# Attention with its first four steps pinned to program order on two engines, its loads in another order, and GpSimd's weight preparation cut into 256-column pieces

## The chip, the cores and the metric

The kernel runs on one core of a Trainium2 chip. The core has five engines that run side by side and wait for each other by semaphores: TensorE (PE; its weight loads stand in rows of their own as PEld), VectorE (DVE), ScalarE (ACT), GpSimd (POOL) and SyncE (SP), which here only issues transfers. The metric is the device time of one execution in microseconds, the median of several.

## The reference, cut to what matters

Attention with sinks and a window, then two mixtures of experts, one after the other, all in float32:

```python
# attention: B, H, S, D = 2, 8, 768, 64; n_sink = 4, window = 128
scores = scale * (q @ k.T)
keep = (pos[None, :] < n_sink) | ((rel >= 0) & (rel < window))
a = softmax(where(keep, scores, -1e9));  x = a @ v          # 1536 tokens of 512
# first mixture: each token goes to one of 8 experts, greedily by its logit, 192 tokens an expert
out[mask] = relu(x[mask] @ w1[e]) @ w2[e]
# second mixture: every token through every expert, weighted by P from 8 Sinkhorn rounds
out += P[:, e:e + 1] * (relu(x @ w1[e]) @ w2[e])
```

## The kernel before

**Attention** works on 12 chunks of 128 tokens (6 for each of two batches) in 15 steps `c`. A step works on four chunks at once, each at another stage. For chunk `c`, PE multiplies queries with keys (`scores`, tile S, 8 heads as two halves of two head pairs) and DVE adds the mask and takes the maximum (`negmax` closes the step). For chunk `c-1`, ACT takes the exponential in place (`expo`, tile pb). For chunk `c-2`, PE transposes the exponentials (`pt`, PSUM tile PT, copied by ACT to the tile pt) and multiplies them with the values (`pv`, PSUM tile o) for the first two head pairs. For chunk `c-3`, `pv` does the other two pairs, ACT copies the sum (`xt`), and `xn` multiplies with an identity that carries the gate's weights (tile xr). In the same step `turn(c+1, "k")` and `turn(c+1, "q")` transpose the next chunk's keys and queries on PE, through one PSUM buffer with the tag "tr" that `turn`, the sinks and the first half of `xn` share. ACT copies the keys out of it (tile KT), DVE the queries (qt).

A scheduler puts the instructions of each engine in an order of its own choice, by its own estimates; the program text gives the dependences and the priority alone. Each engine then works through its own list strictly in that order.

`load(c)` has SP issue three transfers of 256 KB for chunk c: keys, queries, values. Keys and queries have 3 buffers each, values 5. `load_sinks(b)`, in the steps 1 and 7, loads the values of the four sink tokens and makes of them (a matmul by `spread`, a product and three copies on DVE) the tile vs, which chunk 2 of a batch is the first to use. Ahead of all of them on SP stands the gate of the second mixture, wg2.

**Routing and the first mixture** follow: 8 rounds that each choose an expert and its tokens, gather them and run the expert (`moe1`, lines 736 and 747). At the end of a round `operands` makes the sums T1 to T4 and splits each of them into a high and a low part (lines 699 to 707). DVE does the sums and the low parts, each with two inputs in SBUF.

**The second mixture** walks over 32 pieces of weights ("chunks" `(e, i)`) with two token blocks each: 64 units. `first(u)` makes the hidden values by seven products (tiles X, Y, Z; `hidden`, tile h), `second(u-1)` the outputs (tile pa), alternately on PE. `prepare(e, i)` fetches a piece's weights and splits them into a high part by ACT and a low part by POOL. It is a generator that is stepped between the products. Its subtractions on POOL are one of 512, one of 256 and two of 1024 columns for each piece (lines 460 and 477); before them come four small ones of 256 columns (lines 462 to 465, tile S). During the first units the Sinkhorn rounds run too (lines 808 to 819): DVE sums rows, PE sums columns (tile gmx), DVE scales.

```python
        def parts(o, n, x):
            nc.scalar.activation(w1[0][:, o:o + n], x, AF.Copy)
            nc.gpsimd.tensor_sub(w1[1][:, o:o + n], x, w1[0][:, o:o + n].bitcast(F32))
```

Of the kernel before, what the change touches and what calls it, by code (L numbers as in the profile page):

```python
# [8 lines left out]
F32 = mybir.dt.float32  # L9
# [3 lines left out]
AF = mybir.ActivationFunctionType  # L13
# [7 lines left out]
def kernel(  # L21
# [16 lines left out]
    nc = tc.nc  # L38
    B, H, S, D = q.shape
    N, DM = out.shape  # L40
    E = moe_w_gate.shape[1]
    F = moe_w1.shape[2]
    P = 128
    NI = S // P
    NCH = N // P
    NP = H // 2
# [26 lines left out]

    rcx = ExitStack()
    rp = rcx.enter_context(tc.tile_pool(name="rt", bufs=1, side="right"))
    nc.sync.dma_start(wg2, moe2_w_gate.rearrange("(k p) e -> p k e", p=P))
    nc.vector.memset(ones, 1.0)
    NC2 = NCH // 2
    ji = rp.tile([P, NC2 * P], I32, name="ji", tag="row")
# [44 lines left out]
    def attention():  # L124
# [8 lines left out]

        KT = [ap.tile([P, NP, NI, RW], F32, name=f"KT{b}", bufs=1) for b in range(B)]

        def load(c):
            b, i = divmod(c, NI)
            for name, store, src in (("kn", KN, k), ("qn", QN, q), ("vn", VN, v)):
                t = ap.tile([P, H, D], F32, name=name, bufs=5 if name == "vn" else 3)
                nc.sync.dma_start(t, src[b, :, i * P:(i + 1) * P, :].rearrange("h s d -> s h d"))  # L140
                store[c] = t

        SB_ = 4
        load(0)
        load(1)
        load(2)
        identr = ap.tile([P, P], F32R, name="identr", bufs=1)
        nc.vector.tensor_copy(identr, ident)

# [42 lines left out]
                       channel_multiplier=0)  # L192
        nc.vector.tensor_scalar(spread, jr[:NS, :P], pf[:NS, 0:1], None, op0=OP.is_equal)

        def load_sinks(b):

            vn = ap.tile([NS, H, D], F32, name="vsn")
            nc.sync.dma_start(vn, v[b, :, 0:NS, :].rearrange("h s d -> s h d"))
            pt = pp.tile([P, DM], F32, name="tr", bufs=1)
            nc.tensor.matmul(pt, spread, vn.rearrange("s h d -> s (h d)"), start=True, stop=True)  # L200
            vf = ap.tile([P, DM], F32, name="vf", tag="vf", bufs=1)
            nc.vector.tensor_mul(vf, pt, diag)
            t = VS[b] = ap.tile([P, DM], F32R, name="vs")
            nc.vector.tensor_copy(t, vf)
            for g in (1, 3):
                r = slice(g * H * NS, (g + 1) * H * NS)
                nc.vector.tensor_sub(t[r], vf[r], t[r].bitcast(F32))

        def turn(c, which):

            b, i = divmod(c, NI)
            x = (QN if which == "q" else KN).pop(c)
            pt = pp.tile([P, NP, P], F32, name="tr", bufs=1)
            for hp in range(NP):
                nc.tensor.transpose(pt[:, hp, :], x[:, 2 * hp:2 * hp + 2, :].rearrange("p s d -> p (s d)"), ident)  # L215
            if which == "q":
                QT[c] = ap.tile([P, NP, P], F32, name="qt")
                nc.vector.tensor_copy(QT[c], pt)
            else:
                nc.scalar.activation(KT[b][:, :, i, :P], pt, AF.Copy)  # L220
                nc.vector.tensor_copy(KT[b][:, :, i, P:], KT[b][:, :, 0, 0:NS])

        def dims(c):
# [3 lines left out]
        def scores(c, hp):  # L227
            i, nt, w = dims(c)
            if hp == 0:
                NB[c] = ap.tile([P, 4, H], F32, name="nb", bufs=4)  # L230
                PB[c] = ap.tile([P, H, 2 * RW], F32, name="pb", bufs=3)
            mask = M0 if i == 0 else (M1 if i == 1 else M2).rearrange("p t j -> p (t j)")
            ps = [pp.tile([P, 512], F32, name="S", bufs=SB_) for _ in range(2)]

            for s in range(2):
                r = slice(s * D, (s + 1) * D)
                kk = KT[c // NI][r, hp, i, :P] if i == 0 else \
                    KT[c // NI][r, hp, i - 1:i + 1, :].rearrange("p t j -> p (t j)")
                nc.tensor.matmul(ps[s][:, :w], QT[c][r, hp, :], kk, start=True, stop=True)  # L239
            for s in range(2):  # L240
                h = 2 * hp + s
                nc.vector.tensor_tensor_reduce(PB[c][:, h, :w], ps[s][:, :w], mask, scale=1.0, scalar=-3.0e38,  # L242
                                               op0=OP.add, op1=OP.max, accum_out=NB[c][:, 0, h:h + 1])

        def negmax(c, h0=0, h1=H):
            nb = NB[c]
            nc.vector.tensor_scalar(nb[:, 0, h0:h1], nb[:, 0, h0:h1], -scale, None, op0=OP.mult)  # L247

        def expo(c, hp):
            i, nt, w = dims(c)  # L250
            for h in (2 * hp, 2 * hp + 1):
                nc.scalar.activation(PB[c][:, h, :w], PB[c][:, h, :w], AF.Exp, bias=NB[c][:, 0, h:h + 1], scale=scale,  # L252
                                     accum_out=NB[c][:, 2, h:h + 1])

        def recip(c):
            nb = NB[c]
# [5 lines left out]
        def pt_sinks(c):  # L262
            i, nt, w = dims(c)
            if i < 2:
                return
            sp = PB[c][:, :, w - NS:].unsqueeze(1).to_broadcast([P, 2, H, NS])
            sb = ap.tile([P, 2, 2, H, NS], F32R, name="psn")
            nc.vector.tensor_copy(sb[:, 0], sp)
            nc.vector.tensor_sub(sb[:, 1], sp, sb[:, 0].bitcast(F32))
            pm = pp.tile([P, 4, P], F32R, name="PT", bufs=2)  # L270
            nc.tensor.transpose(pm[:, 0, :], sb.rearrange("p a b h j -> p (a b h j)"), identr)
            PS[c] = ap.tile([P, P], F32R, name="pst")
            nc.vector.tensor_copy(PS[c], pm[:, 0, :].bitcast(F32))

        def sinks(c):

            OT[c] = pp.tile([P, NP, P], F32, name="o", bufs=1)
            if c % NI >= 2:
                for hp in range(NP):
                    nc.tensor.matmul(OT[c][:, hp, :], VS[c // NI][:, hp * P:(hp + 1) * P], PS[c], start=(hp == 0),  # L280
                                     stop=False, skip_group_check=True)

        def pt(c, hp):
            i, nt, w = dims(c)
            pm = pp.tile([P, 4, P], F32, name="PT", bufs=2)
            for s in range(2):
                for t in range(nt):
                    nc.tensor.transpose(pm[:, s * nt + t, :], PB[c][:, 2 * hp + s, t * RW:t * RW + P], ident)  # L288
            PT[c, hp] = ap.tile([P, 4, P], F32, name="pt", bufs=4)
            nc.scalar.activation(PT[c, hp][:, :2 * nt], pm[:, :2 * nt], AF.Copy)  # L290

        def pv(c, hp):
            i, nt, w = dims(c)
            b = c // NI
            o = OT[c]
            for t in range(nt):
                for s in range(2):
                    nc.tensor.matmul(o[s * D:(s + 1) * D, hp, :], VN[c - nt + 1 + t][:, 2 * hp + s, :],  # L298
                                     PT[c, hp][:, s * nt + t, :], start=(i < 2 and t == 0), stop=(t == nt - 1),
                                     skip_group_check=True)  # L300

        def xt(c):
            XT[c] = ap.tile([P, NP, P], F32, name="xt")
            nc.scalar.activation(XT[c], OT[c], AF.Copy)

        def xn(c):

# [2 lines left out]
            for h0 in range(0, H, 4):  # L310
                pt_ = pp.tile([P, 2, P + 2 * E], F32, name="xr", **(dict(tag="PT", bufs=2) if h0 else dict(tag="tr", bufs=1)))
                for a in range(2):
                    nc.tensor.matmul(pt_[:, a], XT[c][:, h0 // 2 + a, :], wbd[:, h0 // 2 + a], start=True, stop=True)  # L313
                den = NB[c][:, 3, h0:h0 + 4].rearrange("p (a s) -> p a s", s=2).unsqueeze(3)
                nc.vector.tensor_mul(lp[:, h0:h0 + 4].rearrange("p (a s) e -> p a s e", s=2),
                                     pt_[:, :, P:].rearrange("p a (s e) -> p a s e", s=2),
# [54 lines left out]
        masks()  # L371
        for c in range(NCH + 3):
            c1, c2, c3 = (c - j if 0 <= c - j < NCH else None for j in (1, 2, 3))
            cur = c < NCH
            if c + 3 < NCH:
                load(c + 3)
            if c % NI == 1 and cur:
                load_sinks(c // NI)
            if c2 is not None:
                recip(c2)  # L380
# [32 lines left out]
                        first_round(c3)  # L413
            if cur and c < NCH - 1:
                negmax(c)
        first_count()
        return cx

# [26 lines left out]
    def prepare(e, i):  # L445
# [11 lines left out]

        def parts(o, n, x):
            nc.scalar.activation(w1[0][:, o:o + n], x, AF.Copy)  # L459
            nc.gpsimd.tensor_sub(w1[1][:, o:o + n], x, w1[0][:, o:o + n].bitcast(F32))  # L460

        nc.gpsimd.tensor_add(S[:, 0], A21, A22)
        nc.gpsimd.tensor_sub(S[:, 1], S[:, 0], A11)
# [10 lines left out]
        nc.sync.dma_start(r2, moe2_w2[e, fs, :].rearrange("(k p) d -> p k d", p=P))  # L474
        w2 = bp.tile([P, 2, FP, DM], F32R, name="w2", tag="w", bufs=WB)
        nc.scalar.activation(w2[:, 0], r2, AF.Copy)  # L476
        nc.gpsimd.tensor_sub(w2[:, 1], r2, w2[:, 0].bitcast(F32))  # L477
        WC[e, i] = w1, w2

    def run(steps):  # L480
# [307 lines left out]
    def moe2(cx):  # L788
# [132 lines left out]
        for n in range(len(units) + 1):  # L921
# [8 lines left out]
            for k in (5, 2):  # L930
                for _ in range(k):
                    next(a, None)
                    if n > 1:
                        next(sk, None)
                next(prep, None)
                for j in range(TB):
                    next(b, None)
                    if n > 1:
                        next(sk, None)
                    if j < 2:  # L940
                        next(prep, None)

    cx = routing_and_moe1()
# [35 lines left out]
```

## Time and profile before

| | us |
|---|---|
| median of 3 runs | 1403.85 |
| lowest and highest | 1403.66, 1405.28 |
| the profiled execution, its own time | 1406.31 |
| its span, from the first to the last instruction | 1404.6 |
| attention, about | 0 to 145 |
| routing and the first mixture, about | 145 to 386 |
| second mixture, about | 386 to 1404 |

The profile is of one execution. 1.7 us of its time lie outside of the span. It took 2.5 us longer than the median run, 0.18%. A row of the timeline gives the start, the duration, the engine, the source line and the tiles (out<-in); "[1.18 <-DVE qt L218]" behind it is the time for which the engine stood idle before it, and what ended that.

### The profile page before, as it was taken

The page shows a single profiled execution, that of the slowest core. Times are in us where ns is not written, and L with a number is a line of the kernel's source. Part 1 is how long each engine was busy: PE and PEld are TensorE (multiplying, and loading weights), DVE is VectorE, ACT ScalarE, POOL GpSimd, SP SyncE. Part 2 cuts the span into 40 slices and gives each one's busy share as a digit, 9 for nine tenths or more (in the row PEclk, how much of TensorE's full clock was granted, in tenths as well). Part 3 has the DMA queues.
Part 4 walks back from the last instruction along what each step waited for, and adds up shares of the span by engine and source line. Part 5 has one row for each costly group of instructions (what it writes and reads, how often), then busy time and mean ns, then how long its engine had stood idle before and what let it go on. Part 6 is the DMA issues. An engine that isn't in the chain of part 4 may idle for free.

```text
span 1404.6 us, 20726 instructions
## 1 busy us (share of the span) xinstructions
PE 1361.5 (97%) x8195; PEld 1220.9 (87%) x8195; DVE 810.7 (58%) x1921; ACT 458.5 (33%) x975; POOL 405.4 (29%) x388
## 2 busy tenths in 40 slices
PE   7999599999989999999999999999999999999998
PEld 4677499999988989998999899988998999989987
DVE  4777778860357655555555555555555555555554
ACT  4766111222343333333323233323232333232321
POOL 1146301011342222232333223323332233233203
PEclk8999699999999999999999999999999999999999
DMA  5431434668210000011010000110100001011002
GB/s 122 112 78 39 147 132 154 225 184 225 77 46 30 31 31 31 30 35 42 30 45 31 31 31 30 40 36 31 45 31 30 31 30 44 32 31 45 1 1 90
DMA packets 87225, 87.37 MB, mean 62 GB/s; under 512 B 43864, under 2 KB 60248, under 8 KB 87128
## 3 DMA queue, kind: packets, MB, share of 16 engines
q1 hardware_dynamic: 82056, 73.45, 17.0%
q0 software_dynamic: 2944, 9.44, 1.9%
q10 hardware_dynamic: 2128, 3.16, 0.6%
q8 instruction: 64, 1.05, 0.3%
q14 instruction: 33, 0.27, 0.1%
HBM read 79.75 MB, written 6.30 MB: 61 GB/s over the span
## 4 chain that ended last, share of the span: by engine, by line
PE 90%; DVE 4%; ACT 2%; POOL 2%; issue 1%; POOLq 0%; DVEq 0%; ACTq 0%
PE pa L895 36%; PE X L838 19%; PE Z L838 9%; PE mm L736 6%; PE mm L747 6%; PE Y L838 5%; PE S L239 2%; ACT pb L252 1%; PE o L298 1%; PE cnt L584 1%; PE PT L288 1%; POOL G L355 1%; PE tr L215 1%; PE xr L313 1%; DVE pb L242 1%
## 5 line engine op out<-in xcount | busy, mean ns | idle before, releaser
L895 PE MATMUL pa<-w,h 128*128 128x512 f32 x2304 | 548.7, 391 | 0.0
L895 PEld LDWEIGHTS pa<-w,h 128*128 128x128 f32 x2304 | 430.3, 188 | 85.0
L906 DVE SCALAR_TENSOR_TENSOR accs<-pa,Pm,accs 128x512 f32<-128x512 f32 x360 | 270.1, 750 | 135.0 <-PE pa L895 133.2
L477 POOL TENSOR_TENSOR w<-r,w 128x1024 fp32r<-128x1024 f32 x32 | 77.1, 2409 | 392.1 <-ACT w L476 392.1
L846 DVE SCALAR_TENSOR_TENSOR h<-sum,h 128x384 fp32r<-128x384 f32 x192 | 128.4, 669 | 58.2 <-ACT h L845 58.1
L845 ACT ACTIVATE h<-sum 128x384 fp32r<-128x384 f32 x192 | 100.5, 523 | 158.8 <-DVE sum L855 158.8
L460 POOL TENSOR_TENSOR w1l<-r,w1h 128x512 fp32r<-128x512 f32 x64 | 64.3, 1026 | 294.1 <-ACT w1h L459 285.3
L845 ACT ACTIVATE h<-X 128x384 fp32r<-128x384 f32 x64 | 31.5, 492 | 214.2 <-PE X L838 214.2
L736 PE MATMUL mm<-xe,wf 128*128 128x192 f32 x512 | 95.9, 337 | 0.0
L855 DVE TENSOR_TENSOR sum<-Z,u 128x384 f32<-128x384 f32 x64 | 35.7, 558 | 104.4 <-ACT u L850 104.4
L747 PE MATMUL mm<-hT,wf 128*128 128x192 f32 x512 | 91.5, 331 | 0.0
L855 DVE TENSOR_TENSOR sum<-Y,p 128x384 f32<-128x384 f32 x64 | 35.7, 557 | 89.1 <-PE Y L838 89.1
L460 POOL TENSOR_TENSOR w1l<-S,w1h 128x1024 fp32r<-128x1024 f32 x32 | 86.6, 2707 | 0.0
L736 PEld LDWEIGHTS mm<-xe,wf 128*128 128x128 f32 x512 | 83.2, 192 | 0.1
L747 PEld LDWEIGHTS mm<-hT,wf 128*128 128x128 f32 x512 | 82.6, 190 | 0.5
L846 DVE SCALAR_TENSOR_TENSOR h<-X,h 128x384 fp32r<-128x384 f32 x64 | 35.7, 558 | 53.8 <-ACT h L845 53.8
L850 ACT ACTIVATE p<-X 128x384 f32<-128x384 f32 x64 | 31.5, 491 | 107.2 <-PE X L838 105.4
L684 POOL DMA_INDIRECT xg<-X,ixs x16 | 16.4, 1023 | 168.6 <-PE mm L720 60.6
L850 ACT ACTIVATE u<-X 128x384 f32<-128x384 f32 x64 | 31.5, 493 | 100.9 <-PE X L838 100.9
L476 ACT ACTIVATE w<-r 128x1024 fp32r<-128x1024 f32 x32 | 34.0, 1062 | 88.1 <-PE pa L895 88.1
L252 ACT ACTIVATE pb<-pb,nb 128x264 f32<-128x264 f32 (+1 forms) x96 | 46.3, 486 | 14.1 <-DVE nb L247 14.1
L738 ACT ACTIVATE hT<-mm 128x384 f32<-128x384 f32 x32 | 15.7, 491 | 78.7 <-PE mm L736 78.6
(282 smaller groups left out, 2324.7 us busy)
## 6 DMA issues: line engine op xcount, KB each, us to landing
r<-in_moe_w_dram SPq DMA_DIRECT2D x64, 512.0 KB, 3.4
wf<-in_moe_w_dram SPq DMA_DIRECT2D x29, 1024.0 KB, 7.8
kn<-in_k_dram SPq DMA_DIRECT2D x12, 256.0 KB, 3.9
qn<-in_q_dram SPq DMA_DIRECT2D x12, 256.0 KB, 2.9
vn<-in_v_dram SPq DMA_DIRECT2D x12, 256.0 KB, 3.4
X<-xs POOLq DMA_DIRECT2D x12, 256.0 KB
wf<-in_moe_w_dram ACTq DMA_DIRECT2D x3, 1024.0 KB, 10.4
xg<-X,ixs POOLq DMA_INDIRECT x16
```

The source lines that it names most:

```text
L252: nc.scalar.activation(PB[c][:, h, :w], PB[c][:, h, :w], AF.Exp, bias=NB[c][:, 0, h:h + 1], scale=scale, accum_out=NB[c][:, 2, h:h + 1])
L460: nc.gpsimd.tensor_sub(w1[1][:, o:o + n], x, w1[0][:, o:o + n].bitcast(F32))
L477: nc.gpsimd.tensor_sub(w2[:, 1], r2, w2[:, 0].bitcast(F32))
L736: nc.tensor.matmul(ph[:, j - j0, :], w1[j // JH][:, k, j % JH * P:(j % JH + 1) * P], xe[:, k, :], start=(k == 0), stop=(k == KD - 1))
L747: nc.tensor.matmul(py[:, k - k0, :], w2[j // JH][:, j % JH, k * P:(k + 1) * P], hT[:, j, :], start=(j == 0), stop=(j == KF - 1))
L838: nc.tensor.matmul(acc_, w1[a][:, o, k, :], XO[x][t][b][:, k, :], start=(start and n == 0), stop=(stop and n == 3 * KH - 1), skip_group_ch ...
L845: nc.scalar.activation(t[:, 0], x, AF.Relu)
L846: nc.vector.scalar_tensor_tensor(t[:, 1], x, 0.0, t[:, 0].bitcast(F32), op0=OP.max, op1=OP.subtract)
L850: nc.scalar.activation(t, x, AF.Copy)
L855: nc.vector.tensor_add(t, a, b)
L895: nc.tensor.matmul(pa, HT[u, f, h][:, a, j * P:(j + 1) * P], w2[:, b, f, :], start=(n == 0), stop=(n == 3 * FP - 1))
L906: nc.vector.scalar_tensor_tensor(acc[:, c], pa, pe, acc[:, c], op0=OP.mult, op1=OP.add)
```

## The change

Five things change. (1) In the steps 0 to 3 each instruction of PE and ACT gets an ordering edge to the one that the program issued before it on that engine (`inorder`), so that in these steps both follow the program text; from step 4 on the scheduler is free again. (2) The loads: keys and queries of chunks 0 and 1 go first, the values of a chunk one place later, and wg2 after the values of chunk 2. (3) The queries of chunk 0 are transposed into a buffer of the tag "S" and not into the one that the keys stand in. (4) The sinks' load is issued in the steps 0 and 6 and their matmul and DVE work move to the end of steps 3 and 9 (`make_sinks`). (5) POOL's subtractions in `prepare` go in pieces of 256 columns, 11 where there were 4; and `prepare` isn't stepped in the first unit.

```diff
-        load(0)
-        load(1)
-        load(2)
+        load(0, "kq")
+        load(1, "kq")
+        load(0, "v")
+        load(2, "kq")
+        load(1, "v")
+        load(2, "v")
+        nc.sync.dma_start(wg2, moe2_w_gate.rearrange("(k p) e -> p k e", p=P))
...
+        FILL = 3
+        last = {}
+
+        def inorder(op):
+            i = op.ins
+            if i.engine in last:
+                if last[i.engine] is not None:
+                    tc.add_manual_dep(i, last[i.engine].name, mybir.DependencyInfo(
+                        mybir.DependencyClass.NoSync, mybir.DependencyReason.DATA), reason="in order")
+                last[i.engine] = i
+
+        last.update({mybir.EngineType.PE: None, mybir.EngineType.Activation: None})
...
-            pt = pp.tile([P, NP, P], F32, name="tr", bufs=1)
+            pt = pp.tile([P, NP, P], F32, name="tr", **(dict(tag="S", bufs=SB_) if c == 0 and which == "q" else
+                                                        dict(tag="tr", bufs=1)))
...
+            if c > FILL:
+                last.clear()
...
-            if c % NI == 1 and cur:
+            if c % NI == 0 and cur:
                 load_sinks(c // NI)
...
+            if c % NI == 3 and cur:
+                make_sinks(c // NI)
...
-            nc.gpsimd.tensor_sub(w1[1][:, o:o + n], x, w1[0][:, o:o + n].bitcast(F32))
+            for j in range(n):
+                nc.gpsimd.tensor_sub(w1[1][:, o + j], x[:, j], w1[0][:, o + j].bitcast(F32))
...
-        nc.gpsimd.tensor_sub(w2[:, 1], r2, w2[:, 0].bitcast(F32))
+        for f in range(FP):
+            for h in range(2):
+                d = slice(h * DM // 2, (h + 1) * DM // 2)
+                nc.gpsimd.tensor_sub(w2[:, 1, f, d], r2[:, f, d], w2[:, 0, f, d].bitcast(F32))
...
-                next(prep, None)
+                if n:
+                    next(prep, None)
```

PE in attention, from the second half of the scores of chunk 0 on. Before:

```order
L239 MATMUL S<-KT_126,qt 128x128 x4
L215 MATMUL tr<-ident,qn 128x128 x4
L288 MATMUL PT<-ident,pb 128x128
L239 MATMUL S<-KT_126,qt 128x264 x8
L288 MATMUL PT<-ident,pb 128x128 x3
L298 MATMUL o<-pt,vn 64x128 x2
```

Now:

```order
L263 MATMUL S<-KT_125,qt 128x128 x4
L239 MATMUL tr<-ident,qn 128x128 x4
L263 MATMUL S<-KT_125,qt 128x264 x4
L239 MATMUL tr<-ident,kn 128x128 x4
L263 MATMUL S<-KT_125,qt 128x264 x4
L239 MATMUL tr<-ident,qn 128x128 x4
L263 MATMUL S<-KT_125,qt 128x264 x4
L239 MATMUL tr<-ident,kn 128x128 x4
L312 MATMUL PT<-ident,pb 128x128 x4
```

The transposes of chunk 2's keys and queries and the scores of chunk 2 stood behind all of chunk 0's and most of chunk 1's later work and behind the sinks' matmul; now they come directly after the scores of chunk 1.

ACT over the same steps (KT is the copy of a chunk's keys, pb the exponentials, pt the copy of transposed ones, xt that of a chunk's sum). Before:

```order
L220 ACTIVATE KT_126<-tr 128x4x128 x2
L252 ACTIVATE pb,nb<-pb,nb 128x128 x8
L290 ACTIVATE pt<-PT 128x256 x2
L252 ACTIVATE pb,nb<-pb,nb 128x264 x8
L290 ACTIVATE pt<-PT 128x256 x2
L304 ACTIVATE xt<-o 128x512
```

Now:

```order
L244 ACTIVATE KT_125<-tr 128x4x128 x2
L276 ACTIVATE pb,nb<-pb,nb 128x128 x4
L244 ACTIVATE KT_125<-tr 128x4x128
L276 ACTIVATE pb,nb<-pb,nb 128x128 x4
L276 ACTIVATE pb,nb<-pb,nb 128x264 x4
L244 ACTIVATE KT_125<-tr 128x4x128
L314 ACTIVATE pt<-PT 128x256 x2
L276 ACTIVATE pb,nb<-pb,nb 128x264 x4
L314 ACTIVATE pt<-PT 128x256 x2
L328 ACTIVATE xt<-o 128x512
```

The eight exponentials of chunk 1 stood in one block ahead of the second copy of chunk 0's transposes; now they stand in two blocks of four, with the copies between them.

POOL, the second piece of weights of the second mixture, about where the first mixture ends. Before:

```order
L460 TENSOR_TENSOR w1l<-S,w1h 128x1024
L462 TENSOR_TENSOR S<-r_5122 128x256
L464 TENSOR_TENSOR S<-r_5122 128x256
L463 TENSOR_TENSOR S<-S,r_5122 128x256
L465 TENSOR_TENSOR S<-r_5122,S 128x256
L477 TENSOR_TENSOR w_4939<-r_4937,w_4939 128x1024
```

Now:

```order
L489 TENSOR_TENSOR w1l<-S,w1h 128x256 x4
L491 TENSOR_TENSOR S<-r_5136 128x256
L493 TENSOR_TENSOR S<-r_5136 128x256
L492 TENSOR_TENSOR S<-S,r_5136 128x256
L494 TENSOR_TENSOR S<-r_5136,S 128x256
L509 TENSOR_TENSOR w_5051<-r_5049,w_5051 128x256 x4
```

The sequence is the same, with four short subtractions in the place of each long one. Behind attention the lists of PE, ACT, DVE and SP are the same as before, in the first unit of the second mixture too.

## Rows read from the trace of the kernel before

**Rows 1.** The page, its head.
```profile
span 1404.6 us, 20726 instructions
```
**Rows 2.** Windows: length, busy PE, PEld, DVE, ACT, POOL, PE's granted clock, DMA share, GB/s.
```profile
530.00:1000.00 470.00, 470.00 (x2353) 424.72 (x2352) 257.87 (x393) 146.82 (x271) 149.11 (x120) 1.00 0.10 34
```
**Rows 3.** Waits of PE: us in total, times, longest us.
```profile
PE Y L838 <- DVE sum L855: 4.2, 1, 4.2
...
PE o L298 <- ACT pt L290: 3.1, 1, 3.1
...
PE gmx L816 <- DVE cs L812: 2.2, 2, 1.5
```
**Rows 4.** Windows of attention's first steps.
```profile
20.00:25.00 5.00, 1.91 (x15) 1.34 (x14) 0.38 (x2) 4.05 (x17) 0.00 (x0) 0.72 0.00 0
25.00:30.00 5.00, 5.00 (x19) 2.61 (x18) 1.46 (x3) 1.59 (x3) 0.00 (x0) 0.50 0.00 0
```
**Rows 5.** Timeline of attention's first steps, SP, PE, DVE and ACT.
```profile
0.81 0.44 SPq L76 DMA_DIRECT2D wg<-in_moe_w_gate_dram  x1
1.30 0.50 SPq L140 DMA_DIRECT2D kn<-in_k_dram  x1
...
4.94 1.08 PE L215 MATMUL tr<-ident,kn 128*128 128x128 f32 x4 [4.94 <-POOL jr L187]
...
6.71 1.11 PE L215 MATMUL tr<-ident,qn 128*128 128x128 f32 x4 [0.69 <-ACT KT L220]
...
7.86 0.69 DVE L218 COPY qt<-tr 128x512 f32<-128x512 f32 x1 [0.61 <-PE tr L215]
...
13.22 0.39 ACT L252 ACTIVATE pb<-pb,nb 128x128 f32<-128x128 f32 x1
...
13.86 4.26 PE L239 MATMUL S<-KT,qt 64*128 64x264 f32 x16
...
25.90 0.60 ACT L290 ACTIVATE pt<-PT 128x512 f32<-128x512 f32 x1 [0.50 <-PE PT L288]
...
44.95 1.16 PE L239 MATMUL S<-KT,qt 64*128 64x264 f32 x8
...
53.85 0.71 PE L239 MATMUL S<-KT,qt 64*128 64x264 f32 x2
```
**Rows 6.** The chain that ended last, attention's first steps: start, us, what.
```profile
19.34 3.98 ACT pb L252 x16
```
**Rows 7.** Timeline of PE where the sinks of batch 1 stand now.
```profile
76.08 1.12 PE L200 MATMUL tr<-vsn,spread 4*128 4x512 f32 x2
```
**Rows 8.** The chain that ended last, the second mixture's first units.
```profile
387.34 2.65 DVE T L701
389.99 1.02 DVE T L702
...
394.04 2.61 DVE xT4l L707
...
449.29 2.40 DVE h L846
```
**Rows 9.** Timeline of POOL and DVE over the same units.
```profile
386.89 2.69 POOL L460 TENSOR_TENSOR w1l<-S,w1h 128x1024 fp32r<-128x1024 f32 x1
...
390.56 1.05 POOL L464 TENSOR_TENSOR S<-r 128x256 f32<-128x256 f32 x1
...
398.08 0.56 DVE L846 SCALAR_TENSOR_TENSOR h<-sum,h 128x384 fp32r<-128x384 f32 x1 [0.59 <-ACT h L845]
...
418.99 0.74 POOL L464 TENSOR_TENSOR S<-r 128x256 f32<-128x256 f32 x1
...
448.88 2.40 POOL L460 TENSOR_TENSOR w1l<-S,w1h 128x1024 fp32r<-128x1024 f32 x1
```
**Rows 10.** Windows of the clock in the second mixture's first units.
```profile
397.00:402.00 5.00, 4.46 (x16) 4.31 (x17) 1.43 (x4) 1.78 (x4) 0.00 (x0) 0.66 0.52 106
455.00:460.00 5.00, 4.90 (x20) 4.90 (x21) 4.07 (x12) 1.01 (x2) 0.00 (x0) 0.66 0.01 3
```

More of the change, by code (lines that the diff above doesn't have):

```diff
@@ L75 @@
     rp = rcx.enter_context(tc.tile_pool(name="rt", bufs=1, side="right"))
-    nc.sync.dma_start(wg2, moe2_w_gate.rearrange("(k p) e -> p k e", p=P))
     nc.vector.memset(ones, 1.0)
@@ L134, in attention, with load @@
         KT = [ap.tile([P, NP, NI, RW], F32, name=f"KT{b}", bufs=1) for b in range(B)]
-        def load(c):
+        def load(c, kinds="kqv"):
             b, i = divmod(c, NI)
             for name, store, src in (("kn", KN, k), ("qn", QN, q), ("vn", VN, v)):
+                if name[0] not in kinds:
+                    continue
                 t = ap.tile([P, H, D], F32, name=name, bufs=5 if name == "vn" else 3)
@@ L193, in attention, with make_sinks @@
         nc.vector.tensor_scalar(spread, jr[:NS, :P], pf[:NS, 0:1], None, op0=OP.is_equal)
+        VSN = {}
         def load_sinks(b):
-            vn = ap.tile([NS, H, D], F32, name="vsn")
-            nc.sync.dma_start(vn, v[b, :, 0:NS, :].rearrange("h s d -> s h d"))
+            VSN[b] = ap.tile([NS, H, D], F32, name="vsn")
+            nc.sync.dma_start(VSN[b], v[b, :, 0:NS, :].rearrange("h s d -> s h d"))
+        FILL = 3
[8 more added lines that the diff above has]
+        last.update({mybir.EngineType.PE: None, mybir.EngineType.Activation: None})
+        def make_sinks(b):
+            vn = VSN.pop(b)
             pt = pp.tile([P, DM], F32, name="tr", bufs=1)
-            nc.tensor.matmul(pt, spread, vn.rearrange("s h d -> s (h d)"), start=True, stop=True)
+            inorder(nc.tensor.matmul(pt, spread, vn.rearrange("s h d -> s (h d)"), start=True, stop=True))
             vf = ap.tile([P, DM], F32, name="vf", tag="vf", bufs=1)
@@ L212, in turn @@
             x = (QN if which == "q" else KN).pop(c)
-            pt = pp.tile([P, NP, P], F32, name="tr", bufs=1)
+            pt = pp.tile([P, NP, P], F32, name="tr", **(dict(tag="S", bufs=SB_) if c == 0 and which == "q" else
+                                                        dict(tag="tr", bufs=1)))
             for hp in range(NP):
-                nc.tensor.transpose(pt[:, hp, :], x[:, 2 * hp:2 * hp + 2, :].rearrange("p s d -> p (s d)"), ident)
+                inorder(nc.tensor.transpose(pt[:, hp, :], x[:, 2 * hp:2 * hp + 2, :].rearrange("p s d -> p (s d)"), ident))
             if which == "q":
@@ L219, in turn @@
             else:
-                nc.scalar.activation(KT[b][:, :, i, :P], pt, AF.Copy)
+                inorder(nc.scalar.activation(KT[b][:, :, i, :P], pt, AF.Copy))
                 nc.vector.tensor_copy(KT[b][:, :, i, P:], KT[b][:, :, 0, 0:NS])
@@ L238, in scores @@
                     KT[c // NI][r, hp, i - 1:i + 1, :].rearrange("p t j -> p (t j)")
-                nc.tensor.matmul(ps[s][:, :w], QT[c][r, hp, :], kk, start=True, stop=True)
+                inorder(nc.tensor.matmul(ps[s][:, :w], QT[c][r, hp, :], kk, start=True, stop=True))
             for s in range(2):
@@ L251, in expo @@
             for h in (2 * hp, 2 * hp + 1):
-                nc.scalar.activation(PB[c][:, h, :w], PB[c][:, h, :w], AF.Exp, bias=NB[c][:, 0, h:h + 1], scale=scale,
-                                     accum_out=NB[c][:, 2, h:h + 1])
+                inorder(nc.scalar.activation(PB[c][:, h, :w], PB[c][:, h, :w], AF.Exp, bias=NB[c][:, 0, h:h + 1], scale=scale,
+                                     accum_out=NB[c][:, 2, h:h + 1]))
         def recip(c):
@@ L270, in pt_sinks @@
             pm = pp.tile([P, 4, P], F32R, name="PT", bufs=2)
-            nc.tensor.transpose(pm[:, 0, :], sb.rearrange("p a b h j -> p (a b h j)"), identr)
+            inorder(nc.tensor.transpose(pm[:, 0, :], sb.rearrange("p a b h j -> p (a b h j)"), identr))
             PS[c] = ap.tile([P, P], F32R, name="pst")
@@ L279, in sinks @@
                 for hp in range(NP):
-                    nc.tensor.matmul(OT[c][:, hp, :], VS[c // NI][:, hp * P:(hp + 1) * P], PS[c], start=(hp == 0),
-                                     stop=False, skip_group_check=True)
+                    inorder(nc.tensor.matmul(OT[c][:, hp, :], VS[c // NI][:, hp * P:(hp + 1) * P], PS[c], start=(hp == 0),
+                                     stop=False, skip_group_check=True))
         def pt(c, hp):
@@ L287, in pt @@
                 for t in range(nt):
-                    nc.tensor.transpose(pm[:, s * nt + t, :], PB[c][:, 2 * hp + s, t * RW:t * RW + P], ident)
+                    inorder(nc.tensor.transpose(pm[:, s * nt + t, :], PB[c][:, 2 * hp + s, t * RW:t * RW + P], ident))
             PT[c, hp] = ap.tile([P, 4, P], F32, name="pt", bufs=4)
-            nc.scalar.activation(PT[c, hp][:, :2 * nt], pm[:, :2 * nt], AF.Copy)
+            inorder(nc.scalar.activation(PT[c, hp][:, :2 * nt], pm[:, :2 * nt], AF.Copy))
         def pv(c, hp):
@@ L297, in pv @@
                 for s in range(2):
-                    nc.tensor.matmul(o[s * D:(s + 1) * D, hp, :], VN[c - nt + 1 + t][:, 2 * hp + s, :],
+                    inorder(nc.tensor.matmul(o[s * D:(s + 1) * D, hp, :], VN[c - nt + 1 + t][:, 2 * hp + s, :],
                                      PT[c, hp][:, s * nt + t, :], start=(i < 2 and t == 0), stop=(t == nt - 1),
-                                     skip_group_check=True)
+                                     skip_group_check=True))
         def xt(c):
             XT[c] = ap.tile([P, NP, P], F32, name="xt")
-            nc.scalar.activation(XT[c], OT[c], AF.Copy)
+            inorder(nc.scalar.activation(XT[c], OT[c], AF.Copy))
         def xn(c):
@@ L312, in xn @@
                 for a in range(2):
-                    nc.tensor.matmul(pt_[:, a], XT[c][:, h0 // 2 + a, :], wbd[:, h0 // 2 + a], start=True, stop=True)
+                    inorder(nc.tensor.matmul(pt_[:, a], XT[c][:, h0 // 2 + a, :], wbd[:, h0 // 2 + a], start=True, stop=True))
                 den = NB[c][:, 3, h0:h0 + 4].rearrange("p (a s) -> p a s", s=2).unsqueeze(3)
@@ L939, in moe2 @@
                         next(sk, None)
-                    if j < 2:
+                    if n and j < 2:
                         next(prep, None)
```

## The prediction, made before the run

> **What bounds the kernel now.** I read the page's head first (a span of 1404.6 us [rows 1]), then windows by stage, then PE's waits, and only then the timeline. In the second mixture PE has no gap: it is busy for 470.00 of 470 us from 530 to 1000 [rows 2]. So time can only be won or lost there if PE is made to wait, and no edit takes work from PE. The reader should look at PE's own waits. Most of the long ones lie where this change acts: 3.1 us in attention, on ACT's copy pt; 4.2 us in the first unit of the second mixture, on DVE's sum; 2.2 us in two waits of the Sinkhorn rounds for DVE's column sums [rows 3]. Each has a second price, which is no wait: after it PE's granted clock falls to 0.50, the level of 1.2 GHz, for some us [rows 4]. Its matmuls then take nearly twice as long and look busy.
>
> **Attention before.** The scores of chunk 1 begin at 13.86, those of chunk 4 at 44.95 [rows 5]: 31.1 us for three steps that hold less work than a late one, and the step that begins at 44.95 takes 8.9. The reason stands in the chain: ACT does all eight exponentials of chunk 1 (19.34 to 23.32) [rows 6] before it copies the transposes that PE waits for. PE is idle for 3.1 us, its clock goes to 0.50, and from 25 to 30 it is "busy" at that level [rows 3, 4], with the sinks' matmul among it.
>
> **Attention now, worked out step by step.** Start: wg2's issue ahead of the first keys goes, 1.30 − 0.81 = 0.49. The queries' transposes began at 6.71, when ACT had emptied the one buffer; they can now begin when the keys' end, 4.94 + 1.08 = 6.02, if the queries have landed: 0.69 more [rows 5]. Together 1.2 us for the first scores. The next chain (two halves of scores, two turns) keeps most of it; I take 1.0, so chunk 1's scores begin at 12.9.
>
> Now I follow the pinned lists, whichever engine ends last. As slow as in the rows of the start, four transposes take 1.1 (at 6.71) and half of a chunk's scores 4.26/2 = 2.1; ACT's 512-column copies (KT, pt, xt) take 0.6, one of half that size I put at 0.3; an exponential of chunk 0 0.39, of a later chunk 3.98/8 = 0.50 (the chain counts each with its read-out) [rows 5, 6].
> - Step 1, from 12.9: PE half of scores 2.1, key transposes 1.1, other half 2.1, query transposes 1.1; then DVE's copy qt 0.69 [rows 5]. 7.1, so step 2 begins at 20.0. ACT must hold the second half of chunk 0's exponentials until the keys' copy is done (16.1 + 0.6), 4 × 0.39 = 1.6, done at 18.3: hidden.
> - Step 2: ACT sets the end. Exponentials 2.0, keys 0.6, two short copies 0.6, exponentials 2.0; then DVE, in whose list the first part of the reciprocal, which needs all eight sums, stands ahead of qt: 0.2 + 0.7. 6.1, so step 3 begins at 26.1.
> - Step 3: PE scores 1.16 and the last products of chunk 0, about 0.5; ACT xt 0.6, exponentials 2.0, keys 0.6, two copies 1.2, exponentials 2.0 beside which PE does products, transposes and the first half of xr, about 1.1 more until the next scores. 9.1, so chunk 4's scores begin at 35.2, 9.8 earlier than before.
>
> Here PE is taken to be at the higher level from step 2 on, since step 1 keeps it busy for 6.4 us on end.
>
> What is owed then: half of chunk 1's products with the values, about 0.6, which the list before had done by 44.95; and the sinks, whose matmul holds PE for 1.1 where it stood in batch 1 [rows 7]. Their other move, step 7 to step 9, takes 1.1 out and puts it back. So attention wins 9.8 − 0.6 − 1.1 = 8.1. From step 4 on PE has few gaps, routing needs attention's last logits, and the first mixture's weights are fetched by expert number, after routing; so I carry it to the end unshortened. For sinks the loads come in steps 0 and 6, three steps ahead of need; wg2 is needed only after routing: nothing. Values one place later (about 1.1 us of transfer each) land before 14, and chunk 0's are first used after 22: nothing; if a value tile were late, PE would wait in step 2 behind it, at most by 1.
>
> **The second mixture's start.** At 387.34 a DVE sum T takes 2.65 in the chain, and at 394.04 a low part takes 2.61 [rows 8]. Both lie under one long POOL subtraction (386.89, 2.69) [rows 9] or its like; both have two inputs in SBUF. Between them DVE's same operations take 1.02 from start to start, while POOL runs 256-column operations that themselves take 1.05 [rows 8, 9]: the two alternate. After the change all of POOL's operations there have that size, so six DVE operations take 6 × 1.02 in place of 2.65 + 4 × 1.01 + 2.61: 3.2 us sooner, and PE's wait of 4.2 shrinks to 1.0. Then the clock: over the 5 us after that wait it is 0.66 of full [rows 10], which costs 5 × 0.34 = 1.7; this comes back if the short wait doesn't lower it. Sum 4.9.
>
> The Trainium skill, page "SBUF — State Buffer", section "Who interferes with whom", says that a DVE instruction with two SBUF inputs and a GpSimd instruction exclude each other for the whole instruction. By it, alternating operations would add up, 0.56 for DVE's alone and 0.74 for POOL's alone [rows 9]: 1.30 a pair; six would take 7.8, this term would be 3.2 and the time 1390. The measured 1.02 of the same operations decides.
>
> The second place is DVE's h at 449.29: 2.40 under a POOL subtraction of 2.40 [rows 8, 9]. With pieces it takes 1.02, 1.4 less; the small Sinkhorn operations around it lose a little, since POOL works longer. I take 1.3 of PE's 2.2 [rows 3], and again 5 × 0.34 = 1.7 for the clock after it [rows 10]. Sum 3.0.
>
> Elsewhere pieces cost nothing: a long subtraction becomes four of at most 1.05, some 2 us more POOL time in two units of 16 us (1018 us over 64), where POOL is busy for a third [rows 2]. If the low parts came too late PE would wait on them; they are done a unit ahead. Stepping `prepare` one unit later changes no list: nothing.
>
> **Sum:** 8.1 + 4.9 + 3.0 = 16.0. Against the span 1404.6 that is 1388.6, against the execution's own 1406.3 it is 1390.3; the median run was 2.5 below the profiled one, so I forecast 1403.85 − 16.0 = **1387.8 us**.
>
> **Rivals.**
> (a) *PE stays at the lower level through steps 2 and 3.* The pinned lists make PE wait for ACT in both. At that level scores take 0.9 more a half; each set of transposes I estimate at 0.5 more (half of the start's 1.1), products as much: about 8 us for two steps, of which the gaps absorb half. Attention wins 4, the time is 1392. For it: in rows 4 it sat at 0.50 while busy. Against: gaps worked out here are near 1 us, that one 3.1.
> (b) *The written order takes the gain back.* ACT idles in the lists, some 2 us before the copy of chunk 2's keys and 2 before xt; if each further hand-over costs as much, steps 2 and 3 take 10 us each and more, attention wins 2 and the time is 1394. Against: the later steps, bound by the same hand-overs, take about 9.
> (c) *Pieces don't do what they are for:* POOL holds on through a run of four, DVE waits as long as before. Only attention wins: 1396. Against: the alternation in rows 8 and 9.
> (d) *Slower.* In the second mixture's steady part each piece blocks a two-input DVE operation, more often than one long one did; if DVE's h came late by 0.3 us of PE's time in each of 62 units, 18.6 us would go, more than all gains: 1406. Against: there PE has no gap now and DVE is busy for 55% [rows 2]; it decides only if h has less slack than one piece, some 1 us.
>
> **How the numbers follow.** Forecast, give or take 3.5 (the start 0.6 either way, the second fall of the clock 1.7, hand-overs 1 each): 0.56. (a) 0.18, (b) 0.14, (c) 0.09, (d) 0.03. The range of 8 in 10 goes from 1383.5, all terms at their upper ends, to 1396, which holds (a), (b) and most of (c). About 0.2% (2.8 us) is what a measurement of this kernel tells from no change. All but (d) end below 1401: faster 0.94; between its price and the gains lies little, same 0.03, slower 0.03.
>
> **What would show it.** Chunk 4's scores near 35; no window at 0.50 between 20 and 33; ACT's exponentials in fours. Around 379, DVE's T and low parts at about 1.0, none at 2.6; PE's wait for sum near 1.0; granted clock 1.00 after it; likewise for h near 435. PE still without a gap in the steady units. If chunk 4's scores come after 39 with the clock at 0.50, (a); with it at 1.00, (b). If DVE's long ones stay, (c).

## The result and the profile after

The changed kernel takes 1388.73 us in the median (1387.02 to 1390.14) against 1404.57 for the kernel before, four executions of each, a ratio of 0.9883 (interval 0.9871 to 0.9896). The forecast was 1387.8, in a range from 1383.5 to 1396. The profiled execution took 1387.89 us.

The waits of PE show first what is gone (columns: what waits, for what, us in total, times, longest):

```profile
PE S L263 <- DVE qt L242: 4.0, 4, 1.2
...
PE Y L870 <- DVE sum L887: 1.6, 1, 1.6
PE o L322 <- ACT pt L314: 1.1, 1, 1.1
...
PE gmx L848 <- DVE cs L844: 0.3, 1, 0.3
```

The three waits of [rows 3] have shrunk, 4.2 to 1.6, 3.1 to 1.1 and 2.2 to 0.3. Of the four waits for DVE's copy of the queries one was there before, ahead of chunk 0's scores (0.8); three are new, at the start of steps 1 to 3 as the prediction followed them. The windows at about the same places of the program (columns as in rows 2):

```profile
20.00:25.00 5.00, 3.87 (x39) 2.54 (x36) 3.56 (x17) 2.92 (x12) 0.00 (x0) 1.00 0.91 205
25.00:30.00 5.00, 3.91 (x39) 3.02 (x40) 2.15 (x13) 4.97 (x17) 0.00 (x0) 1.00 0.26 58
385.00:390.00 5.00, 5.00 (x28) 4.79 (x29) 3.00 (x6) 1.93 (x5) 2.51 (x4) 1.00 0.27 78
435.00:440.00 5.00, 5.00 (x28) 4.41 (x27) 3.86 (x13) 0.72 (x2) 4.84 (x8) 1.00 0.28 105
520.00:990.00 470.00, 470.00 (x2353) 424.69 (x2352) 261.03 (x393) 147.45 (x272) 166.72 (x225) 1.00 0.11 35
```

The reader should look at the sixth figure behind the window's length, PE's granted clock: 1.00 in all five, where [rows 4, 10] had 0.72, 0.50, 0.66 and 0.66. And the last row has no gap of PE in the steady units, with POOL at 166.72 us in place of 149.11.

Attention's scores, in PE's timeline (start, duration):

```profile
12.45 1.16 PE L263 MATMUL S<-KT,qt 64*128 64x264 f32 x8 [0.78 <-DVE qt L242]
...
17.21 1.16 PE L263 MATMUL S<-KT,qt 64*128 64x264 f32 x8 [1.17 <-DVE qt L242]
...
23.23 1.16 PE L263 MATMUL S<-KT,qt 64*128 64x264 f32 x8 [1.13 <-DVE qt L242]
...
31.82 0.71 PE L263 MATMUL S<-KT,qt 64*128 64x264 f32 x2
```

These are the first scores of chunks 1 to 4; those of chunk 4 begin 13.1 us earlier than in [rows 5]. At the second mixture's start DVE and POOL read so:

```profile
375.86 1.11 DVE L732 TENSOR_TENSOR T<-yT,T 128x384 f32<-128x384 f32 x1 [3.50 <-ACT yT L781]
376.89 1.08 DVE L733 TENSOR_TENSOR T<-yT 128x384 f32<-128x384 f32 x1
377.90 1.09 DVE L734 TENSOR_TENSOR T<-yT,T 128x384 f32<-128x384 f32 x1
...
381.95 1.08 DVE L739 TENSOR_TENSOR xT4l<-T,xT4h 128x384 fp32r<-128x384 f32 x1
...
383.32 0.55 DVE L887 TENSOR_TENSOR sum<-Y,p 128x384 f32<-128x384 f32 x1
...
433.86 0.82 DVE L878 SCALAR_TENSOR_TENSOR h<-sum,h 128x384 fp32r<-128x384 f32 x1
```
```profile
376.50 4.10 POOL L489 TENSOR_TENSOR w1l<-S,w1h 128x256 fp32r<-128x256 f32 x4
```

No DVE operation takes 2.6 any more: each of the sums and low parts begins 1.01 to 1.03 behind the one before it, while POOL does its four pieces in 4.10. The h that took 2.40 [rows 8] takes 0.82.

### The profile page after: what moved, and what is told of

It reads as the page before. It is cut to its first block, busy times and chain, and to the rows that moved or that the text cites. A ratio compares the mean times of both kernels' runs of the same rounds, so it can differ in the third digit from the quotient of the medians.

```text
span 1386.2 us, 20957 instructions
## 1 busy us (share of the span) xinstructions
PE 1349.7 (97%) x8195; PEld 1213.9 (88%) x8195; DVE 811.0 (59%) x1921; ACT 458.2 (33%) x975; POOL 443.3 (32%) x612
## 4 chain that ended last, share of the span: by engine, by line
PE 92%; DVE 4%; ACT 2%; issue 1%; POOL 1%; DMA 0%; POOLq 0%; SPq 0%; DVEq 0%; ACTq 0%
PE pa L927 37%; PE X L870 19%; PE Z L870 9%; PE mm L768 6%; PE mm L779 6%; PE Y L870 5%; PE S L263 2%; ACT pb L276 1%; PE o L322 1%; PE cnt L616 1%; PE PT L312 1%; PE xr L337 1%; DVE pb L266 1%; PE tr L239 1%; POOL out_dram L940 1%
## 5 line engine op out<-in xcount | busy, mean ns | idle before, releaser
L509 POOL TENSOR_TENSOR w<-r,w 128x256 fp32r<-128x256 f32 x128 | 90.4, 739 | 365.8 <-ACT w L505 365.8
L878 DVE SCALAR_TENSOR_TENSOR h<-sum,h 128x384 fp32r<-128x384 f32 x192 | 136.4, 711 | 58.1 <-ACT h L877 57.9
L489 POOL TENSOR_TENSOR w1l<-r,w1h 128x256 fp32r<-128x256 f32 x96 | 68.6, 743 | 275.1 <-ACT w1h L487 267.1
L489 POOL TENSOR_TENSOR w1l<-S,w1h 128x256 fp32r<-128x256 f32 x128 | 102.7, 832 | 0.0
```

The lines of the kernel that those rows point to most:

```text
L489: nc.gpsimd.tensor_sub(w1[1][:, o + j], x[:, j], w1[0][:, o + j].bitcast(F32))
L509: nc.gpsimd.tensor_sub(w2[:, 1, f, d], r2[:, f, d], w2[:, 0, f, d].bitcast(F32))
L878: nc.vector.scalar_tensor_tensor(t[:, 1], x, 0.0, t[:, 0].bitcast(F32), op0=OP.max, op1=OP.subtract)
```

## The experiments

Each was timed beside the kernel before on the same chip. The first four take the change apart.

**Whole subtractions again.** The changed kernel, with POOL's eleven pieces as four operations.

```diff
-            for j in range(n):
-                nc.gpsimd.tensor_sub(w1[1][:, o + j], x[:, j], w1[0][:, o + j].bitcast(F32))
+            nc.gpsimd.tensor_sub(w1[1][:, o:o + n], x, w1[0][:, o:o + n].bitcast(F32))
...
+        nc.gpsimd.tensor_sub(w2[:, 1], r2, w2[:, 0].bitcast(F32))
```

> The changed kernel with GpSimd's subtractions of the weight preparation whole again (512, 256, 1024, 1024 columns); attention stays as changed. Theory (DVE's two-input operations wait for a long POOL operation to end): the two waits at the start of the second mixture come back, so about 7 us of the 16 go: 1396, PE's wait for sum near 4, a DVE sum T and a low part at 2.6, the granted clock 0.50 after it. Rival (they met only because attention ended at an unlucky moment, and the earlier end of attention alone parts them): no DVE operation over 1.1, the time stays near 1389.

1395.36, ratio 0.9929 (0.9916 to 0.9943) to the kernel before. The waits came back (waits of PE, then DVE's timeline, then two windows):

```profile
PE Y L866 <- DVE sum L883: 4.2, 1, 4.2
...
PE gmx L844 <- DVE cs L840: 2.2, 2, 1.5
```
```profile
377.57 2.73 DVE L729 TENSOR_TENSOR T<-yT 128x384 f32<-128x384 f32 x1
...
384.27 2.69 DVE L735 TENSOR_TENSOR xT4l<-T,xT4h 128x384 fp32r<-128x384 f32 x1
```
```profile
385.00:390.00 5.00, 2.15 (x7) 2.15 (x8) 3.32 (x5) 1.28 (x3) 1.54 (x1) 0.77 0.50 106
446.00:451.00 5.00, 5.00 (x28) 4.70 (x27) 4.57 (x12) 1.85 (x4) 0.00 (x0) 1.00 0.01 3
```

So an earlier end of attention doesn't part the two engines; the pieces do. But the last window, right behind the wait of 1.5 for the column sums, is at 1.00, where [rows 10] had 0.66 behind the same wait.

**Pieces alone.** The kernel before with the pieces of the change and nothing else.

> The kernel before with the subtractions in pieces of 256 columns and nothing else. Theory: 7 us faster, 1397, all of it between the first sum T of the second mixture and its fourth unit; attention as before. Rival (the gain of the pieces hangs on the other edits): under 2 us faster, 1402 or more.

1397.99, ratio 0.9952 (0.9938 to 0.9965): 6.2 us by the medians. PE waits for sum for 1.6 us and for the column sums for 0.3, as in the changed kernel. The pieces need nothing of the other edits.

**No ordering edges.** The changed kernel without the line that switches them on.

```diff
-        last.update({mybir.EngineType.PE: None, mybir.EngineType.Activation: None})
```

> The changed kernel without the ordering edges; loads, buffer, moved sinks and pieces stay. Theory as predicted (the pinned order wins in attention): most of attention's gain goes, 1396 or more, chunk 4's scores after 40. Rival (the sinks' matmul, which waited for a late load with the one buffer that the transposes need, was what held the order back, and its move alone lets the scheduler find nearly the written order): within 2 us of the changed kernel, 1387 to 1391, chunk 4's scores between 31 and 35.

1388.67, ratio 0.9886 (0.9871 to 0.9901), the same as the changed kernel. PE's timeline, chunks 1 and 4:

```profile
11.74 1.16 PE L262 MATMUL S<-KT,qt 64*128 64x264 f32 x8
...
31.31 0.71 PE L262 MATMUL S<-KT,qt 64*128 64x264 f32 x2
```

The scheduler, left free, is no later than the written order. My theory of the pins falls here. The rival's time and its mark in the trace are met; that the sinks' move is the reason is for the next run to show.

**The sinks' move alone.** The kernel before, with the sinks' load and matmul moved and nothing else.

```diff
-            if c % NI == 1 and cur:
+            if c % NI == 0 and cur:
                 load_sinks(c // NI)
...
+            if c % NI == 3 and cur:
+                make_sinks(c // NI)
```

> The kernel before with the sinks' load and matmul moved and nothing else: no ordering edges, old order of loads, old buffer, whole subtractions. Theory as predicted (the sinks' move costs and gains nothing, the pins bring the gain): 1402 to 1405. Rival (the move alone brings most of attention's gain): 1393 to 1396, chunk 4's scores before 37, no stretch at a granted clock of 0.50 between 20 and 33.

1395.72, ratio 0.9937 (0.9924 to 0.9951): 8.5 us by the medians. PE's timeline and the windows that were at 0.72 and 0.50 [rows 4]:

```profile
13.87 1.16 PE L258 MATMUL S<-KT,qt 64*128 64x264 f32 x8 [0.17 <-DVE qt L237]
...
18.67 1.16 PE L258 MATMUL S<-KT,qt 64*128 64x264 f32 x8
...
33.21 0.71 PE L258 MATMUL S<-KT,qt 64*128 64x264 f32 x2
33.85 1.12 PE L219 MATMUL tr<-vsn,spread 4*128 4x512 f32 x2
```
```profile
20.00:25.00 5.00, 3.81 (x31) 2.67 (x29) 3.48 (x19) 4.69 (x20) 0.00 (x0) 1.00 0.72 165
25.00:30.00 5.00, 4.91 (x51) 3.61 (x48) 2.90 (x16) 4.97 (x17) 0.00 (x0) 1.00 0.25 56
```

The edit that the prediction priced at a loss of 1.1 brings attention's gain. This run and the one with whole subtractions differ in the pins, the loads and the buffer of chunk 0's queries alone: 1395.72 and 1395.36. So these three together bring nothing that can be measured once the sinks have moved.

**The pins alone.** The kernel before with the ordering edges and nothing else.

> The kernel before with the ordering edges of steps 0 to 3 and nothing else: the sinks' matmul is pinned in step 1, ahead of chunk 1's scores, and its load is issued near 16.6 as before. Theory as predicted (the pinned order brings the gain by itself): 1394 to 1397. Rival (the pins without the sinks' move make PE stand before chunk 1's scores until the sink values have landed, some 6 us, at the lower clock after it): chunk 1's scores after 18, 1398 to 1404.

1406.2, ratio 1.0008 (0.9999 to 1.0017); the rival's mark in the trace is met (chunk 1's scores after 18), but the time lies above its range too. PE's timeline and windows:

```profile
20.14 2.04 PE L220 MATMUL tr<-vsn,spread 4*128 4x512 f32 x2 [7.14 <-DMA vsn<-in_v_dram]
22.11 2.13 PE L259 MATMUL S<-KT,qt 64*128 64x264 f32 x8
...
43.36 0.71 PE L259 MATMUL S<-KT,qt 64*128 64x264 f32 x2
```
```profile
15.00:20.00 5.00, 0.00 (x0) 0.00 (x0) 0.00 (x0) 0.00 (x0) 0.00 (x0) 0.64 0.93 210
20.00:25.00 5.00, 4.86 (x14) 2.40 (x14) 2.68 (x6) 0.00 (x0) 0.00 (x0) 0.50 0.00 0
```

With the order pinned, PE stands for 7.14 us before the sinks' matmul, because the values of the four sink tokens land only near 20. Then PE runs at 0.50, and the 1.6 us by which chunk 4's scores still come before those of [rows 5] are gone again by routing. In the kernel before, SP's timeline has that load behind the gate and fifteen others:

```profile
16.58 1.51 SPq L198 DMA_DIRECT2D vsn<-in_v_dram  x2
```

And PE's timeline there has the sinks' matmul and the transposes of chunk 2's keys so:

```profile
26.37 2.07 PE L200 MATMUL tr<-vsn,spread 4*128 4x512 f32 x2
...
31.07 1.12 PE L215 MATMUL tr<-ident,kn 128*128 128x128 f32 x4
```

This points to what the scheduler of the kernel before had worked around: it put the sinks' matmul at 26.37, behind the time near 20 at which the values land in the run with the pins, and the transposes of chunk 2, which use the same single buffer after it, later still. The next run tests it.

**The sinks' loads first.** To tell the late load from the matmul's place: the kernel before, with both sink loads right behind the loads of chunk 0; the matmul stays in step 1.

```diff
         load(0)
+        for b in range(B):
+            VSN[b] = ap.tile([NS, H, D], F32, name=f"vsn{b}", bufs=1)
+            nc.sync.dma_start(VSN[b], v[b, :, 0:NS, :].rearrange("h s d -> s h d"))
         load(1)
         load(2)
...
-            vn = ap.tile([NS, H, D], F32, name="vsn")
-            nc.sync.dma_start(vn, v[b, :, 0:NS, :].rearrange("h s d -> s h d"))
+            vn = VSN.pop(b)
```

> The kernel before with the sinks' two loads directly behind the loads of chunk 0, and nothing else: their matmul stays in step 1, ahead of the turning of chunk 2, in the one buffer tr; no pins, whole subtractions. Theory (the buffer is held by a matmul whose values come late, issued at 16.58 behind fifteen loads): with the values there early the scheduler's order is nearly that of the run with the sinks moved, chunk 4's scores before 37, 1394 to 1397. Rival (the matmul's place in step 1 is what does the harm): chunk 4's scores after 42, 1401 to 1405.

1398.36, ratio 0.9954 (0.9941 to 0.9968), 6.0 us by the medians; 1.4 above the theory's range, with its mark in the trace (chunk 4's scores before 37) met:

```profile
13.12 1.12 PE L203 MATMUL tr<-vsn,spread 4*128 4x512 f32 x2
14.18 1.42 PE L242 MATMUL S<-KT,qt 64*128 64x264 f32 x8
...
21.53 1.16 PE L242 MATMUL S<-KT,qt 64*128 64x264 f32 x8
...
34.34 0.71 PE L242 MATMUL S<-KT,qt 64*128 64x264 f32 x2
```

The lateness of the values explains most. The matmul's place costs as well: in step 1 it stands ahead of chunk 1's scores for 1.1 us, and chunk 2's scores begin at 21.53, 2.9 later than with the sinks moved. Whether another buffer for the sinks, or the matmul's move without the load's, would do as well was not tried; that the single buffer is what ties the transposes to the matmul is read from the program and from PE's list.

**Old order of the loads.** The changed kernel with the gate first and each chunk's keys, queries and values together.

> The changed kernel with the gate first and the loads in the old order (keys, queries, values of each chunk); all else as changed. Theory as predicted (0.5 for the gate; values late cost nothing): chunk 0's first transposes near 4.9, chunk 1's scores about 0.6 later than in the changed kernel, 1389 to 1390. Rival (the new order of loads is what brings keys in time for the pinned list): PE waits for keys in steps 1 and 2, 1392 or more.

1388.29, ratio 0.9879 (0.9864 to 0.9894); chunk 1's scores begin at 12.63 against 12.45. The time is 0.7 below the theory's range: a gain of the new order was not to be measured.

**Other sizes of the pieces.** The changed kernel with pieces of 512 and of 128 columns; one of the edits for 128 is shown, for 512 two pieces are taken together.

```diff
             for j in range(n):
-                nc.gpsimd.tensor_sub(w1[1][:, o + j], x[:, j], w1[0][:, o + j].bitcast(F32))
+                for k in range(KH):
+                    nc.gpsimd.tensor_sub(w1[1][:, o + j, k], x[:, j, k], w1[0][:, o + j, k].bitcast(F32))
```

> The changed kernel with pieces of 512 columns. Theory (a two-input DVE operation starts when the POOL operation under way ends; POOL's operations alone take 0.74 for 256 and 1.29 for 512 columns, and the pairs of 256 took 1.02, so a pair of 512 about 1.57): three of the seven DVE operations take 0.55 longer, PE's wait for sum grows from 1.6 to 3.3, and the time by 1.7, or by 3 if the clock falls after it: 1390 to 1392. Rival (only the whole 1024-column operations hurt): 1389.

1390.8, ratio 0.9898 (0.9882 to 0.9913). DVE's timeline:

```profile
376.64 1.63 DVE L732 TENSOR_TENSOR T<-yT 128x384 f32<-128x384 f32 x1
378.19 1.64 DVE L733 TENSOR_TENSOR T<-yT,T 128x384 f32<-128x384 f32 x1
```

> The changed kernel with pieces of 128 columns (22 for each piece of weights). Theory: a pair would take about 0.75 where POOL runs such pieces, PE's wait for sum of 1.6 all but goes: 1387 to 1388. Rival (more pieces block DVE more often, and POOL's fixed cost makes its work longer): steady units show gaps of PE or the wait stays, 1389 or more.

1387.52, ratio 0.9873 (0.9858 to 0.9888):

```profile
378.45 0.81 DVE L734 TENSOR_TENSOR T<-yT 128x384 f32<-128x384 f32 x1
379.18 0.81 DVE L735 TENSOR_TENSOR T<-yT,T 128x384 f32<-128x384 f32 x1
```

From start to start DVE's operation takes 0.73 with pieces of 128, 1.01 with 256, 1.55 with 512 and 2.66 with 1024 columns. With 512 two operations ran at that pace, not the three that I expected, and PE's wait for sum was 2.2, not 3.3; with 128 that wait is not among PE's waits at all.

**Combinations.** The changed kernel without ordering edges and with pieces of 128; the kernel before with two edits only, the sinks' loads first and pieces of 128; and the changed kernel once more.

> The changed kernel without the ordering edges and with pieces of 128 columns. Theory (the edges are worth nothing, 128 in place of 256 saves the last wait for sum, 1.6): 1386.5 to 1387.5, 1 to 1.6 below the changed kernel of the same call. Rival (the wait is replaced by another): the same as the changed kernel within 0.5.

> The kernel before with two edits: the sinks' loads behind those of chunk 0, and pieces of 128 columns. Theory (these two causes carry nearly all of the gain): 8 for attention and 8 for the second mixture, 1387 to 1389.5. Rival (the loads in the new order and the buffer carry a part): 1391 or more.

> The changed kernel once more, to stand beside the two others of this call on the same chip: 1388 to 1390 by every theory.

| | us | ratio to before (interval) |
|---|---|---|
| no edges, pieces of 128 | 1386.87 | 0.9870 (0.9855 to 0.9885) |
| two edits | 1389.15 | 0.9892 (0.9877 to 0.9907) |
| the changed kernel again | 1389.24 | 0.9889 (0.9874 to 0.9904) |

The first is the fastest kernel of the study, 2.4 us below the changed one, more than the 1.6 that I gave as the most; the intervals overlap, so the order of the two is likely rather than settled. The two edits come out at the time of the whole change, but with smaller pieces than it has. Beside the first row, whose pieces are as small, 2.3 us are missing: about the 2.5 by which the sinks' loads alone (6.0) fall short of the sinks' whole move (8.5).

## Why the prediction was right, and where it was not

**The time and the mechanism in the second mixture: right.** The kernel before, DVE's timeline:

```profile
386.69 0.65 DVE L700 TENSOR_TENSOR T<-yT,T 128x384 f32<-128x384 f32 x1 [3.49 <-ACT yT L749]
387.26 2.73 DVE L701 TENSOR_TENSOR T<-yT 128x384 f32<-128x384 f32 x1
...
396.94 0.55 DVE L855 TENSOR_TENSOR sum<-Y,p 128x384 f32<-128x384 f32 x1
```

From the second T to the sum that PE waits for it takes 9.68 us (387.26 to 396.94), the changed kernel 6.43 (376.89 to 383.32): 3.25 for the 3.2 of the prediction. The prediction missed that the first T, free before (0.57 from start to start), now meets a piece as well (1.03). So DVE is 2.8 sooner, and PE's wait shrinks by 2.6, to 1.6 and not to 1.0. The clock behind it gave back 1.3, not 1.7. At the column sums 1.9 came off (2.2 to 0.3) where I took 1.3.

**The second clock term was not to be counted on.** I took 1.7 for it and the two traces show 1.5. But the run with whole subtractions has the same wait of 1.5 and stays at 1.00. Without this term the trace gives 2.6 + 1.3 + 1.9 = 5.8 for the pieces, and the medians give 6.2 (pieces alone) and 6.6 (1395.36 − 1388.73). The prediction's 7.9 for the second mixture (4.9 + 3.0) was thus too large by 1.3 to 1.7.

**Attention: the size about right, the cause wrong.** The step that failed is the one that let the pinned lists make the new order and priced the sinks' move at a loss ("so attention wins 9.8 − 0.6 − 1.1"). The edges are worth nothing where the sinks have moved, and alone they make PE wait for 7.14 us; the sinks' move alone gives 8.5 us. What failed in reading: the sinks' matmul at 26.37 was read as work that costs its 1.1 wherever it stands. It was the mark of a late load: with that load alone moved forward, 6.0 of the 8.5 came. The kernel before held the hint: the sinks' load is issued at 16.58, behind all others, and the transposes of chunk 2 come behind the matmul in PE's list. I took that list for the scheduler's whim. That the sum of 16.0 came so near to the measured 15.8 is in part luck: the move that I had priced at a loss was among the five edits, and a second mixture reckoned 1.3 to 1.7 too high stood beside an attention reckoned 0.4 to 0.7 too low.

**The steps within attention.** Steps 2 and 3 took 6.0 and 8.6, predicted 6.1 and 9.1. Step 1 took 4.8 for 7.1, since its matmuls were fast from 12.45 on (1.16 for eight score matmuls), where I had reckoned with the start's slowness; in the run with pieces of 128, where the same eight took 2.13, it took 6.5 (last section). Routing's first matmul on the tile ch, in the kernel before and in the changed one:

```profile
157.09 1.05 PE L642 MATMUL sm<-ch,oh 128*96 128x4 bf16 x12 [4.63 <-DVE ch L638]
```
```profile
146.08 1.04 PE L674 MATMUL sm<-ch,oh 128*96 128x4 bf16 x12 [4.63 <-DVE ch L670]
```

So of the 13.1 us that chunk 4's scores were ahead, 11.0 were left where routing begins; the 2.1 that went are the 1.7 that I had owed and 0.4 more. By the medians attention's part is 8.5 (sinks alone) to 8.8 (whole subtractions).

**Profiled pair and medians.** The two profiled executions lie 18.4 apart, the medians 15.8. Of the 2.6 between, 1.5 is the clock behind the column sums. The rest fits what executions differ by at the start: the traces with the attention of before reach routing at 157.09 and 156.27 (pieces alone), five with the attention of the changed kernel between 145.90 and 148.17. So attention wins 8.1 to 11.2 by the pair that one takes, and the profiled pair's 11.0 lies near the upper end.

**The waits and the rivals.** I wrote that most of PE's long waits lie where the change acts. The list also has 4.9, 4.6 and 4.5, at the start and in routing, and of these 4.0, 4.6 and 3.9 remain. Neither (a) nor (b) came: PE waits up to 1.2 for the queries' copy, and the granted clock stays at 1.00 through steps 2 and 3. (c) and (d) are excluded by DVE's rows and by 470.00 of 470. The rule of the Trainium skill, page "SBUF — State Buffer", section "Who interferes with whom", by which either of two such instructions holds the port for its whole length, would have given 1.30 a pair. The runs give 0.26 to 0.28 on top of POOL's own time at each size: 0.73, 1.01, 1.55 and 2.66 against the 0.46, 0.74, 1.29 and 2.39 that one such piece takes in the steady units (medians). The rule's direction holds, that the long instruction is waited for to its end; of DVE's 0.56 half is hidden all the same.

## What to carry to other kernels

Where a scheduler's order looks odd, ask which late value and which single buffer it has worked around, before pinning another order: one small load moved forward, and the matmul on it moved back, gave what the pinned order was thought to give, and the pins alone gave nothing. Where the operations of two engines exclude each other by turns, as DVE's and POOL's did here, the one on the path waits for one instruction of the other; so the other's instructions are cut to the size of wait that one can bear, as long as it has idle time for the overhead. And a gain counted from a lower clock behind a wait holds only if the clock falls there in every execution; one trace of a kernel doesn't tell that.

## What the runs showed that was not expected

The clock behind the same waits of PE for the column sums (2.2 in all, the longer one 1.5) fell in two traces and stayed up in three: 0.66 in the kernel before and 0.67 with the pins alone, 1.00 with whole subtractions, with the sinks moved and with the sinks' loads first. The two are the kernels whose attention is not shorter, and each kernel has one trace; so whether the fall goes with the kernel or with the execution stays open. That executions of one kernel differ is on record: in the 33 of the kernel before that were timed beside the experiments the mean granted clock goes from 0.980 to 0.986, and the time from 1406.96 down to 1403.11 with it. Where in the span it differs, those runs don't say.

The start has two faces too. In the run with pieces of 128, whose program is that of the changed kernel up to the weight preparation, PE's timeline reads:

```profile
12.38 2.13 PE L263 MATMUL S<-KT,qt 64*128 64x264 f32 x8 [0.78 <-DVE qt L242]
...
18.92 1.16 PE L263 MATMUL S<-KT,qt 64*128 64x264 f32 x8 [1.23 <-DVE qt L242]
...
33.54 0.71 PE L263 MATMUL S<-KT,qt 64*128 64x264 f32 x2
```

The same eight matmuls took 2.13 here and 1.16 in the changed kernel's profile, and what follows in attention is 1.7 later. Of the five traces with this attention three have 1.16 and two 2.13 (the other is that with whole subtractions). The granted clock reads 1.00 from 12 to 17 in both runs, so the column doesn't show this slowness of the start; the durations do.
